# Several small moves around the attention pieces of a fused sliding-window attention and ELU feed-forward kernel

## The chip, the cores and the metric

One core of a Trainium2 chip runs the whole program. The metric is the device time of one execution in microseconds (us). PE is the matmul engine, DVE the vector engine, ACT the scalar engine, POOL the GpSimd engine and SP the engine that issues the DMAs. [...]

## The reference

```python
# attention: q, k, v are [8 batches, 8 heads, 576, 64]
scores = (q @ k.T) / sqrt(64)
mask   = (0 <= rel < 32)                                # heads 0 to 3
       | (0 <= rel < 128 and rel % 4 == 0)              # heads 4 to 7
attn   = softmax(where(mask, scores, -1e9)) @ v
x      = attn as [4608, 512]                            # 8 batches x 576 rows, 8 heads x 64
# feed-forward
h = x @ w_in                                            # [512, 2048]
g = where(h > 0, h, exp(min(h, 0)) - 1)                 # ELU
out = g @ w_out                                         # [2048, 512]
```

The inputs are float32. The feed-forward products split each operand in a rounded part and a rest (names `xh`, `xl`, `gh`, `gl`, `wh`, `wl`) and add three matmuls.

## The kernel before

**Chunks.** The 4608 rows of x are nine chunks of 512 (`c` = 0 to 8). Chunks 0 to 2 go through sixteen blocks of 128 hidden columns (`f`); I write (c, f) for a place there. Chunks 3 to 8 (`CS` = 3) do the first product by a scheme with seven products for eight: four groups `g` of seven steps `s`, numbered `step = 7 * g + s`.

**A block of chunk 1 or 2.** PE does the first product of block f into a PSUM bank `h0` (12 matmuls of 512 columns), then the second product of block f - 2 into the banks `o_ps` (12 matmuls). There is one `h0`: the next first product waits until ACT has copied `h0` away. The ELU of the block is ACT copy of `h`, ACT exp, ACT relu, DVE scalar_tensor_tensor (e), ACT cast to `gh`, DVE subtraction to `gl`. The last two, "the rest" of the ELU (lines 577 and 578), are asked for one block later (`before`, `steps`). `gl` is read by every third matmul of the second product two blocks on.

**Attention pieces.** Attention for later batches is cut into pieces of two head pairs. A scores piece (`scores_piece`) is 72 small matmuls, which appear as 144 in the trace, into the banks `a_ps0`, `a_ps1` and `h1`. After a third of them ACT reads one column of `h1` into `nothing` (line 481): the second head's scores into that bank wait for this read. Then DVE adds masks, takes the maximum, subtracts; ACT takes exp; DVE sums, scales, and makes six transposes into `pt` for each head pair. An outputs piece (`outputs_piece`) multiplies `pt` with v, one head pair after the other, and ACT copies the outputs to `x32`. In chunks 1 and 2 the pieces stand after the blocks in `WHEN` (scores, outputs, scores, outputs); after block (2, 14) stands one scores piece for chunk 3's group; in chunks 3 to 8 the pieces stand at the steps in `PIECES`.

**What sets the order.** A scheduler orders the instructions of each engine when the program is built, from the order of the code and its own estimate of time; `tc.issue_after` adds an edge. What goes through `vec`, `act` or `inorder` keeps its order in the code: all matmuls, and DVE and ACT from block (2, 14) on. For batches up to `CS` the softmax goes through plain `nc.vector` and `nc.scalar`, and the scheduler places it; for later ones its steps are spread by hand (`work`, `SPARE`). `split_late` (lines 180 and 182) casts and subtracts weights once a block in chunk 1, `combine` (lines 230 to 237) prepares weights for chunk 3 at the places in `COMBINE`. `fifo` and `pop(n)` hold and issue the second products from chunk 3 on; `FIRST_POPS` and `POPS` say how many at a step.

**Shared small buffers.** Four buffers `e` of 128x512 serve the ELU, the output rows (`store`, line 600), and the casts of `combine`; a buffer is free again when its last reader, or the DMA that stores it, is done. `gl` has two buffers, `gh` three.

Of the kernel before, what the change touches and what calls it, by code (L numbers as in the profile page):

```python
# [18 lines left out]
B, H, S, D = 8, 8, 576, 64  # L19
# [5 lines left out]
G = 32  # L25
QB = 3 * G
NU = S // QB
NPAIR = H // 2
NA = 3
GU = QB // G  # L30
# [16 lines left out]
STORED = "A11 A12 S2 S4 S3 S1 A22".split()  # L47
MOVING = "B11 T2 T3 B21 T1 T4 B22".split()
POPS = (3, 4, 0, 4, 0, 5, 0)
FIRST_POPS = (2, 2, 1, 2, 1, 1, 2)  # L50
TODO = [t.split() for t in ("u1 exp0< relu0< rest1< w0", "u2 elu0< cast0< w1", "u3 rest0< w2", "C11 w3", "C22 w4", "C21 exp1 relu1 w5 push1", "elu1 C12 cast1 w6 push0")]
SPARE = ((0.9, 0.3, 1.0, 0.9, 1.2, 2.2, 0.3), (0.9, 0.9, 0.0, 1.6, 2.2, 1.0, 0.3), (0.9, 0.9, 2.2, 1.2, 2.0, 2.4, 0.3), (0.6, 0.6, 0.0, 0.3, 0.6, 1.2, 0.3))
OPERANDS = [t.split() for t in ("", "cast:B11 make:T1", "rest:B11", "make:T2 cast:T2", "rest:T2", "make:T3", "cast:T3 rest:T3",
                                "cast:B21 rest:B21", "make:T4 cast:T1", "rest:T1 cast:T4", "rest:T4 cast:B22", "rest:B22", "", "")]
WHEN = {1: (0, 6, 7, 13), 2: (1, 6, 7, 12)}
EARLY = 0.0
LAST = 14
OPER = 12
PLAIN = ("a5", "a-1'")
COMBINE = {(1, 11): 0, (1, 13): 1, (1, 15): 2, (2, 1): 3, (2, 4): 4, (2, 6): 5, (2, 9): 6, (2, 11): 7}  # L60
PIECES = {9: ("S", 2, 1), 14: ("O", 0, 1), 21: ("O", 2, 1), 23: ("S", 0, 2)}

TINY = float(np.array([0x38000000], np.uint32).view(np.float32)[0])
# [3 lines left out]
def body(ctx: ExitStack, tc: tile.TileContext, q, k, v, masks, w_in, w_out, out):  # L67
# [311 lines left out]
    def exponentials(b, hp, places, sm=None):  # L379

        if sm is None:
            sm = ap.tile([QB, 2 * NU, 2 * G], F32, name="sm", bufs=1)
            last = masks_added(hp, places, sm)
            if b == 1:
                masked.append(last.ins)
        nmx = ap.tile([QB, 2 * NU], F32, name="nmx", bufs=4)
        sums = ap.tile([QB, 2 * NU], F32, name="sums", bufs=4)
        nc.vector.tensor_reduce(out=nmx, in_=sm, op=ALU.max, axis=mybir.AxisListType.X)
        if b == 1:

            maxima.append(nc.vector.tensor_scalar(out=nmx, in0=nmx, scalar1=-0.125, scalar2=None, op0=ALU.mult).ins)
            for u in range(NU):
                exponential(u, sm, nmx, sums)
        else:
            nc.vector.tensor_tensor(out=sm, in0=sm, in1=nmx.unsqueeze(2).broadcast_to([QB, 2 * NU, 2 * G]), op=ALU.subtract)
            nc.scalar.activation(out=sm, in_=sm, func=AF.Exp, scale=0.125)
            nc.vector.tensor_reduce(out=sums, in_=sm, op=ALU.add, axis=mybir.AxisListType.X)
        return b, hp, sm, nmx, sums

    def probabilities(b, hp, sm, nmx, sums):  # L400

        if b == 1:

            for u in range(NU, 2 * NU):
                exponential(u, sm, nmx, sums)
        normalise(nc.vector, sm, sums, lambda ins: ins)
        tr = transposed()
        for c in range(GU):
            for r in range(2):
                ks, cs, rs = slice((c + r) * G, (c + r + 1) * G), slice(c * G, (c + 1) * G), slice(r * G, (r + 1) * G)  # L410
                last_transpose[b] = nc.vector.transpose(out=tr[ks, :, cs], in_=sm[cs, :, rs]).ins
        return b, hp, tr

    def three():

        return banks() + [ps_h.tile([P, TC], F32, name="h1")]
# [49 lines left out]
    def scores_piece(b, hps):  # L466

        s = three()

        def place(j, h, n0, n1):  # L470

            bank, o = (s[h], n0 + j * NU) if j == 0 or n0 < 2 else (s[2], n0 - 2 + h * 4)
            return bank[:, o * 2 * G:(o + n1 - n0) * 2 * G]

        qk = [qk_of.pop(b * NPAIR + hp) for hp in hps]

        one, other = [(0, n) for n in range(NU)], [(1, n) for n in range(NU)]
        for i, (first_head, second_head) in enumerate(zip(other[2:] + other[:2] + one, other[:2] + one + other[2:])):
            if i == 4:

                nc.scalar.copy(out=nothing, in_=place(1, 0, NU - 1, NU)[:QB, 2 * G - 1:])
            for c in range(GU):
                for h, (j, n) in enumerate((first_head, second_head)):
                    score(place(j, h, n, n + 1), *qk[j], h, n, c)
        groups = [[[(n0, n1, place(j, h, n0, n1)) for n0, n1 in (((0, NU),), ((2, NU), (0, 2)))[j]] for h in range(2)] for j in range(2)]
        if b <= CS:
            made = [probabilities(*exponentials(b, hp, groups[j])) for j, hp in enumerate(hps)]
        else:
            made = later_probabilities(b, hps, groups)
        for hp in hps:  # L490
            load_qk(b * NPAIR + hp + 2)
        return made
# [205 lines left out]
    def pop(n):  # L698
        for _ in range(min(n, len(fifo))):
            second_product(*fifo.pop(0))  # L700
# [30 lines left out]
    def combined_chunk(c):  # L731

        x_ps = y_ps = None
        halves = lambda x: x.rearrange("p (i t) -> p i t", i=2)
        for g in range(NG):
            base = (c - CS) * NG * 7 + g * 7
            for s in range(7):
                step = 7 * g + s
                what, hp, ahead = PIECES.get(step, ("", 0, B))
                if what and c + ahead < B:  # L740
                    if what == "S":
                        if hp:
                            work(100.0)
                        made[hp] = scores_piece(c + ahead, (hp, hp + 1))
                    else:
                        if hp:
                            work(100.0)
                        outputs_piece(made.pop(hp))
                        if hp == 0:
                            side.extend(held)  # L750
                            held.clear()
                load_combined(base + s + RING)
                if s == 0:
                    x_ps = ps_h.tile([P, TC], F32, name="h0")
                    live["before"], live["now"] = live.get("now"), (c, g, [sets.pop(0), sets.pop(0)])
                    sets.extend(live["now"][2])
                if (c, g, s) == (CS, 1, 0):
                    moving["temporary"] = late
                if s == 3:
                    y_ps = ps_h.tile([P, TC], F32, name="h1")  # L760
                product(base + s, x_ps if ORDER[s] in ("A11", "S2", "S3", "A22") else y_ps, s in (0, 3, 4))
                for what in TODO[s]:
                    if what in ("u1", "u2", "u3"):
                        live[what] = fp.tile([P, TC], F32, name="e")
                        act.copy(out=live[what], in_=x_ps)
                    elif what == "C21":
                        act.copy(out=rows[1][:, :, :HT], in_=halves(x_ps))
                    elif what[0] == "C":
                        to, u = {"C11": (rows[0][:, :, :HT], "u1"), "C22": (rows[1][:, :, HT:], "u3"), "C12": (rows[0][:, :, HT:], "u2")}[what]
                        vec.tensor_tensor(out=to, in0=halves(y_ps), in1=halves(live.pop(u)), op=ALU.add)  # L770
                    elif what[0] == "w":
                        work(SPARE[g][s])
                    elif what[0] == "p":
                        push(int(what[4:]))
                    else:
                        activation(what)
                if g == NG - 1 and c + 1 < NCH:
                    for what in OPERANDS[s]:
                        moving_operand(c + 1, what, vec, act)
                if g == 0:  # L780
                    for what in OPERANDS[7 + s]:
                        moving_operand(c, what, vec, act)
                pop((FIRST_POPS if (c, g) == (CS, 0) else POPS)[s])

    def second_attention():

# [80 lines left out]
    for c in range(CS):  # L867
# [14 lines left out]
        for f in range(NF):  # L882
# [20 lines left out]
            if c == 0 and f >= NF - 2:  # L903
                ends.append(elu_steps(gemm1(c, f)))
                if f == NF - 2:
                    next(ends[0])
                    first_late = split_steps(0, 0, 2, [slots(*a) for a in LATE[0]], vec, act)
                else:
                    for _ in first_late:
                        pass  # L910
                    next(ends[0])
            else:
                steps = elu(gemm1(c, f), c, f, before, *strict)
                g = next(steps)
                if c == 0 or c == CS - 1 and f >= NF - 3:
                    if g[1] is not None:
                        next(steps)
                    steps = None
                before = steps
                pend.append((c, f, g))  # L920
            if c == 1:
                keep_plain(f)
            if (c, f) == (0, 0):
# [103 lines left out]
```

## Time and profile before

| what | value |
|---|---|
| median of 3 runs | 884.86 us (884.64 to 887.34) |
| the profiled execution's own time | 884.33 us |
| its span, first to last instruction | 882.5 us |
| mean granted PE clock | 0.994 |
| busy in the span: PE, DVE, ACT | 863.4, 609.1, 455.7 us |

PE is busy in nearly all of the span, but its matmuls are pipelined and their ends are modelled, so the times to look at are those between the starts of matmuls, and the few places where PE stands. A row of the timeline gives start, duration, engine, line, operation, names (out<-in), sizes, and in brackets the idle time ahead of it with what ended it.

### The profile page before, as it was taken

To read this page: it belongs to the slowest core of one execution; us is meant where nothing else is said; L and a number is where in the kernel's file an instruction comes from. 1 tells how busy PE (TensorE), PEld (TensorE's weight loads), DVE (VectorE), ACT (ScalarE), POOL (GpSimd) and SP (SyncE) were. 2 spreads that over 40 slices of the span, in tenths; PEclk is the share of its full clock that TensorE was granted. 3 is DMA by queue.
4 is the path that set the end of the run, shared out by engine and by line. 5 is a ranking of instruction groups with operands and counts; after the bars stand their busy time and mean duration, and the time that the engine had idled before them with its cause. 6 is when DMAs were issued, how large, how long until landed. Compare 5 with 4: busy or idle time off the path is not lost. (4 is left out here: it accounts for less than half of the span.)

```text
span 882.5 us, 17850 instructions
## 1 busy us (share of the span) xinstructions
PE 863.4 (98%) x7424; PEld 725.6 (82%) x7424; DVE 609.1 (69%) x921; ACT 455.7 (52%) x783; POOL 6.0 (1%) x12
## 2 busy tenths in 40 slices
PE   6999999999999999999999999999999999999998
PEld 5545678878878888898989998889898989998996
DVE  6999998867588968966867597748775533453332
ACT  3666667645655565434554455446454453454334
POOL 2000000000000000000000000000000000000000
PEclk7999999999999999999999999999999999999999
DMA  9996335123454657757575657656665565557541
GB/s 342 387 356 245 123 121 187 48 92 120 155 199 156 198 165 226 227 187 236 176 258 188 225 178 248 219 182 223 196 199 167 167 215 176 183 175 224 175 144 48
DMA packets 66961, 170.68 MB, mean 193 GB/s; under 512 B 6752, under 2 KB 21440, under 8 KB 66880
## 3 DMA queue, kind: packets, MB, share of 16 engines
q1 hardware_dynamic: 66880, 169.54, 58.9%
q8 instruction: 59, 0.97, 0.4%
q14 instruction: 22, 0.18, 0.1%
HBM read 141.20 MB, written 28.31 MB: 192 GB/s over the span
## 5 line engine op out<-in xcount | busy, mean ns | idle before, releaser
L104 PE MATMUL h<-xh,r 128*128 128x256 f32 (+1 forms) x984 | 223.2, 308 | 2.1 <-PE h L104 1.0
L104 PEld LDWEIGHTS h<-xh,r 128*128 128x128 f32 x984 | 165.1, 191 | 13.9 <-PE h L104 1.2
L104 PE MATMUL h<-xl,r 128*128 128x256 f32 (+1 forms) x492 | 142.7, 307 | 0.6 <-DVE xl L424 0.6
L104 PE MATMUL o_ps<-a,r 128*128 128x512 f32 x480 | 117.0, 391 | 0.0
L424 DVE SCALAR_TENSOR_TENSOR a-1_3249<-a-1_3249,a 128x1024 f32<-128x1024 f32 x48 | 58.7, 1223 | 83.2 <-ACT a L424 83.1
L424 DVE TENSOR_TENSOR a-1_3249<-h,e 128x512 f32<-128x512 f32 x72 | 49.7, 690 | 82.5 <-PE h L104 81.1
L104 PEld LDWEIGHTS h<-xl,r 128*128 128x128 f32 x492 | 93.8, 191 | 9.0 <-issue 2.1
L104 PEld LDWEIGHTS o_ps<-a,r 128*128 128x128 f32 x480 | 87.6, 188 | 16.5
L104 PE MATMUL o_ps<-a,gh 128*128 128x512 f32 x248 | 89.4, 463 | 0.0
L424 ACT COPY e<-h 128x512 f32<-128x512 f32 x72 | 42.2, 586 | 80.8 <-PE h L104 65.7
L104 PE MATMUL h<-a,r 128*128 128x256 f32 x576 | 77.5, 284 | 0.0
L104 PEld LDWEIGHTS h<-a,r 128*128 128x128 f32 x576 | 74.0, 191 | 3.0
L424 ACT COPY a-1_3249<-h 128x512 f32<-128x512 f32 x24 | 14.1, 587 | 109.6 <-PE h L104 109.6
L104 PEld LDWEIGHTS o_ps<-a,gh 128*128 128x128 f32 x248 | 46.3, 188 | 24.2 <-issue 17.2
L424 ACT ACTIVATE a<-a 128x1024 f32<-128x1024 f32 (+1 forms) x56 | 57.0, 1030 | 1.3
L104 PE MATMUL o_ps<-r,r 128*128 128x512 f32 x212 | 56.8, 391 | 0.0
L104 PE MATMUL o_ps<-a,a 128*128 128x512 f32 x216 | 54.6, 391 | 0.0
L424 ACT ACTIVATE a<-a-1_3249 128x1024 f32<-128x1024 f32 x48 | 51.0, 1063 | 1.3 <-DVE a-1_3249 L424 0.5
L104 PEld LDWEIGHTS o_ps<-a,a 128*128 128x128 f32 x216 | 39.4, 188 | 7.4
L424 ACT CAST r<-a-1_3249 128x1024 fp32r<-128x1024 f32 x32 | 33.6, 1050 | 22.2 <-DVE a-1_3249 L424 22.1
L104 PEld LDWEIGHTS o_ps<-r,r 128*128 128x128 f32 x212 | 38.7, 188 | 7.3
L424 DVE TENSOR_TENSOR r<-a-1_3249,r 128x1024 fp32r<-128x1024 f32 x32 | 39.0, 1218 | 6.7 <-ACT r L424 6.2
(179 smaller groups left out, 1431.6 us busy)
## 6 DMA issues: line engine op xcount, KB each, us to landing
r<-combined SPq DMA_DIRECT2D x168, 512.0 KB, 4.1
vt<-v SPq DMA_DIRECT2D x30, 384.0 KB, 4.2
kt<-k SPq DMA_DIRECT2D x30, 304.0 KB, 4.9
out<-e SPq DMA_DIRECT2D x35, 256.0 KB, 3.1
qt<-q SPq DMA_DIRECT2D x30, 288.0 KB, 4.0
r<-w_in SPq DMA_DIRECT2D x16, 512.0 KB, 7.6
r<-w_out SPq DMA_DIRECT2D x16, 512.0 KB, 8.0
combined<-a SPq DMA_DIRECT2D x20, 256.0 KB, 2.9
```

What stands on the lines that cost most here:

```text
L104: return inorder(nc.tensor.matmul(*args, **kw))
L424: return lambda *args, **kw: inorder(getattr(self.eng, name)(*args, **kw))
```

## The change

Five edits, all of order and place; the arithmetic is the same.

1. `WHEN[2]` (1, 6, 7, 12) becomes (2, 6, 7, 12): the first scores piece of chunk 2 stands one block later. In chunk 3 the piece at step 9 moves to step 10, ahead of the product that writes `h1`, with two pops behind it, and the pops of chunk 3's second group change from (3, 4, 0, 4, 0, 5, 0) to (3, 4, 3, 3, 0, 1, 0).
2. For batches up to `CS` a generator `softmax` writes the six transposes as three and three, spread over the blocks behind the piece.
3. At the blocks in `WHEN` the ELU's rest is asked for at once, ahead of the piece, not one block later.
4. In chunk 3, group 0, step 4, the subtraction `rest:B22` (it makes `xl3`) is asked for ahead of that step's other work.
5. The read of `nothing` between the heads goes to DVE, in order, for batches over `CS`: at (2, 14) and in chunks 3 to 6.

```diff
-FIRST_POPS = (2, 2, 1, 2, 1, 1, 2)
+FIRST_POPS = (2, 2, 1, 2, 1, 1, 2), (3, 4, 3, 3, 0, 1, 0)
-WHEN = {1: (0, 6, 7, 13), 2: (1, 6, 7, 12)}
+WHEN = {1: (0, 6, 7, 13), 2: (2, 6, 7, 12)}
+FIRST_PIECES = {10: ("S", 2, 1), 14: ("O", 0, 1), 21: ("O", 2, 1), 23: ("S", 0, 2)}
 PIECES = {9: ("S", 2, 1), 14: ("O", 0, 1), 21: ("O", 2, 1), 23: ("S", 0, 2)}
+    def softmax(b, hp, places, tr):
+        _, _, sm, _, sums = exponentials(b, hp, places)
+        normalise(nc.vector, sm, sums, lambda ins: ins)
+        yield
+        for c in range(GU):
+            for r in range(2):
...
+                last_transpose[b] = nc.vector.transpose(out=tr[ks, :, cs], in_=sm[cs, :, rs]).ins
+                if (c, r) == (1, 0):
+                    yield
+        yield
...
-                nc.scalar.copy(out=nothing, in_=place(1, 0, NU - 1, NU)[:QB, 2 * G - 1:])
+                (vec.tensor_copy if b > CS else nc.scalar.copy)(out=nothing, in_=place(1, 0, NU - 1, NU)[:QB, 2 * G - 1:])
...
-            made = [probabilities(*exponentials(b, hp, groups[j])) for j, hp in enumerate(hps)]
+            trs = [transposed() for _ in hps]
+            made = [(b, hp, tr) for hp, tr in zip(hps, trs)]
+            one, other = [softmax(b, hp, groups[j], trs[j]) for j, hp in enumerate(hps)]
+            next(one)
+            spread.extend(((one,), (one, other), (other,), (other,)))
...
+                        if c == CS and hp:
+                            pop(2)
...
+                if (c, g, s) == (CS, 0, 4):
+                    moving_operand(c, *OPERANDS[7 + s], vec, act)
...
-                pop((FIRST_POPS if (c, g) == (CS, 0) else POPS)[s])
+                pop((FIRST_POPS[g] if c == CS and g < 2 else POPS)[s])
...
+                if steps is not None and f in when:
+                    next(steps)
+                    steps = None
...
+            for steps in spread.pop(0) if spread else ():
+                next(steps)
```

What the built programs then issue, at three places. The numbers of buffers differ between the two programs, and lines behind the edits have moved by up to twenty.

**DVE after block (1, 0).** `e_1373` is that block's ELU and `gl_1380` its rest, `sm_14..` is the first head pair's softmax, `a7` and `a6` are weight rests of `split_late`. Before:

```order
L573 SCALAR_TENSOR_TENSOR e_1373<-h_1374,e_1373 128x512
L375 TENSOR_TENSOR sm_1471<-a_ps1_1396,masks_sb_76 96x384
L375 TENSOR_TENSOR sm_1471<-a_ps0_1395,masks_sb_76 96x384
L388 TENSOR_REDUCE nmx_1474<-sm_1471 96x12
L395 TENSOR_TENSOR sm_1471<-sm_1471,nmx_1474 96x768
```

Now:

```order
L593 SCALAR_TENSOR_TENSOR e_1373<-h_1374,e_1373 128x512
L598 TENSOR_TENSOR gl_1380<-e_1373,gh_1379 128x512
L376 TENSOR_TENSOR sm_1473<-a_ps1_1398,masks_sb_76 96x384
L183 TENSOR_TENSOR a7_1493<-a1_521,a7_1493 128x1024
L183 TENSOR_TENSOR a6_1546<-a1_521,a6_1546 128x1024
L376 TENSOR_TENSOR sm_1473<-a_ps0_1397,masks_sb_76 96x384
L389 TENSOR_REDUCE nmx_1476<-sm_1473 96x12
L396 TENSOR_TENSOR sm_1473<-sm_1473,nmx_1476 96x768
```

The ELU's rest and two weight rests now stand ahead of the second mask and the subtraction; on ACT the exp of `sm` still stands ahead of the copy of the next block's `h0`.

**ACT around the moved scores piece of chunk 2.** `h_2489` is block (2, 2), `e_2488` and `gh_2496` its ELU, `e_2457` the last of four output rows that are copied and stored here, `e_2465` and `e_2470` casts of `combine`. Before, behind block (2, 1):

```order
L572 ACTIVATE e_2426<-e_2426 128x512
L600 COPY e_2451<-o_ps_1605 128x512
L481 COPY nothing_78<-h1_2477 96x1
L600 COPY e_2457<-o_ps_1609 128x512
L236 CAST e_2465<-a5_2125 128x512
```

Now, behind block (2, 2):

```order
L620 COPY e_2457<-o_ps_1603 128x512
L237 CAST e_2465<-a5_2125 128x512
L578 COPY h_2489<-h0_2475 128x512
L597 CAST gh_2434<-e_2426 128x512
L237 CAST e_2470<-a5_2125 128x512
L583 ACTIVATE e_2488<-h_2489 128x512
L592 ACTIVATE e_2488<-e_2488 128x512
L597 CAST gh_2496<-e_2488 128x512
L497 COPY nothing_78<-h1_2518 96x1
L397 ACTIVATE sm_2592<-sm_2592 96x768
```

The read moved from behind block (2, 1)'s relu to behind block (2, 2)'s cast to `gh`. `e_2488` takes the buffer of `e_2457`.

**DVE at the scores piece after (2, 14).** `e_3315` is the block's ELU, the second row its rest. Before:

```order
L424 SCALAR_TENSOR_TENSOR e_3315<-h_3316,e_3315 128x512
L424 TENSOR_TENSOR r3_1227<-e_3315,gh_3321 128x512
L424 TENSOR_TENSOR a5_2125<-h1_3326,masks_sb_76 96x256 x2
L424 TENSOR_TENSOR a5_2125<-a_ps0_3324,masks_sb_76 96x128
L424 TENSOR_TENSOR a5_2125<-a_ps1_3325,masks_sb_76 96x128
```

Now:

```order
L440 SCALAR_TENSOR_TENSOR e_3315<-h_3316,e_3315 128x512
L440 TENSOR_TENSOR r3_1227<-e_3315,gh_3321 128x512
L440 COPY nothing_78<-h1_3326 96x1
L440 TENSOR_TENSOR a5_2125<-h1_3326,masks_sb_76 96x256 x2
L440 TENSOR_TENSOR a5_2125<-a_ps0_3324,masks_sb_76 96x128
```

The read, which stood on ACT between the block's exp and its relu, stands on DVE behind the block's whole ELU.

More of the change, by code (lines that the diff above doesn't have):

```diff
@@ L412, in probabilities @@
         return b, hp, tr
+    spread = []
+    def softmax(b, hp, places, tr):
[4 more added lines that the diff above has]
+            for r in range(2):
+                ks, cs, rs = slice((c + r) * G, (c + r + 1) * G), slice(c * G, (c + 1) * G), slice(r * G, (r + 1) * G)
+                last_transpose[b] = nc.vector.transpose(out=tr[ks, :, cs], in_=sm[cs, :, rs]).ins
+                if (c, r) == (1, 0):
+                    yield
+        yield
     def three():
@@ L738, in combined_chunk @@
                 step = 7 * g + s
-                what, hp, ahead = PIECES.get(step, ("", 0, B))
+                what, hp, ahead = (FIRST_PIECES if c == CS else PIECES).get(step, ("", 0, B))
                 if what and c + ahead < B:
@@ L779, in combined_chunk @@
                         moving_operand(c + 1, what, vec, act)
-                if g == 0:
+                if g == 0 and (c, s) != (CS, 4):
                     for what in OPERANDS[7 + s]:
                         moving_operand(c, what, vec, act)
-                pop((FIRST_POPS if (c, g) == (CS, 0) else POPS)[s])
+                pop((FIRST_POPS[g] if c == CS and g < 2 else POPS)[s])
     def second_attention():
```

## The prediction, made before the changed kernel was run

> **What bounds the kernel now.** I read the page first: busy time per engine and the DMA issues.
>
> ```profile
> PE 863.4 (98%) x7424; PEld 725.6 (82%) x7424; DVE 609.1 (69%) x921; ACT 455.7 (52%) x783; POOL 6.0 (1%) x12
> ...
> out<-e SPq DMA_DIRECT2D x35, 256.0 KB, 3.1
> ```
>
> PE is the bound, and the change adds and removes no matmul. So only places where PE stands can pay, and every new wait of PE is lost in full. Then the waits of PE behind the first 100 us (engine and tile, who released it; total, times, longest):
>
> ```profile
> PE h L104 <- ACT nothing L481: 1.5, 3, 0.9
> PE o_ps L104 <- DVE gl L578: 1.3, 1, 1.3
> PE h L104 <- PE h L104: 1.0, 1, 1.0
> PE h L104 <- issue: 0.9, 1, 0.9
> PE h L104 <- DVE xl L424: 0.6, 1, 0.6
> ```
>
> Seven waits. The timeline of PE has the instructions that ended them:
>
> ```profile
> 195.47 0.50 PE L104 MATMUL o_ps<-a,gl 128*128 128x512 f32 x1 [1.29 <-DVE gl L578]
> ...
> 248.24 0.39 PE L104 MATMUL h<-xh,r 128*128 128x512 f32 x1 [0.95 <-issue]
> ...
> 323.35 0.24 PE L104 MATMUL h<-kt,qt 64*32 64x64 f32 x1 [0.23 <-ACT nothing L481]
> ...
> 343.99 0.39 PE L104 MATMUL h<-xl,r 128*128 128x256 f32 x1 [0.63 <-DVE xl L424]
> ...
> 358.86 0.36 PE L104 MATMUL h<-xh,r 128*128 128x256 f32 x1 [1.01 <-PE h L104]
> ...
> 450.39 0.24 PE L104 MATMUL h<-kt,qt 64*32 64x64 f32 x1 [0.92 <-ACT nothing L481]
> ...
> 635.82 0.24 PE L104 MATMUL h<-kt,qt 64*32 64x64 f32 x1 [0.40 <-ACT nothing L481]
> ```
>
> The brackets understate the loss. A matmul of 512 columns is drawn 0.39 long, but the next starts 0.23 later (below, 12 of them take 249.60 to 252.32, 2.72); the modelled end hides 0.16 of each wait, 0.2 for the small matmuls of scores. So the losses are 1.45, 1.11, 0.43, 0.79, 1.17, 1.12 and 0.60: 6.7 us in all, the most that this change can win. Now what it puts in their place, place by place.
>
> **The piece after (2, 14): +2.8.** The old order, with the durations of one ELU:
>
> ```profile
> 321.90 0.24 PE L104 MATMUL h<-kt,qt 64*32 64x64 f32 x1
> ...
> 322.00 0.59 ACT L424 COPY h<-h 128x512 f32<-128x512 f32 x1 [1.08 <-PE h L104]
> 322.62 0.63 ACT L424 ACTIVATE e<-h 128x512 f32<-128x512 f32 x1
> 323.16 0.14 ACT L481 COPY nothing<-h 96x1 f32<-96x1 f32 x1
> 323.28 0.63 ACT L424 ACTIVATE e<-e 128x512 f32<-128x512 f32 x1
> ...
> 323.94 0.69 DVE L424 SCALAR_TENSOR_TENSOR e<-h,e 128x512 f32<-128x512 f32 x1 [2.29 <-ACT e L424]
> ...
> 324.67 0.62 ACT L424 CAST gh<-e 128x512 fp32r<-128x512 f32 x1 [0.76 <-DVE e L424]
> ...
> 325.32 0.69 DVE L424 TENSOR_TENSOR r<-e,gh 128x512 fp32r<-128x512 f32 x1 [0.69 <-ACT gh L424]
> ```
>
> Scores start at 321.90 and PE restarts at 323.35 after losing 0.43, so the read is wanted 1.0 us after the scores start. Now the read stands on DVE behind the ELU's last subtraction, which ends at 326.01. It can end at about 326.15 (0.14, the price on ACT; DVE's isn't shown, and 0.1 either way changes little). PE restarts 2.8 later than before. ACT is relieved of 0.14 only, so the ELU isn't earlier. Queued behind the read on DVE are the masks, wanted by nobody on PE soon. This is the surest term; it would shrink only if DVE's order were another.
>
> **The piece after (1, 0): +1.5.**
>
> ```profile
> 138.10 1.05 ACT L180 CAST r<-a 128x1024 fp32r<-128x1024 f32 x1
> ...
> 139.99 0.58 ACT L558 COPY h<-h 128x512 f32<-128x512 f32 x1
> 140.32 1.22 DVE L182 TENSOR_TENSOR a<-a,a 128x1024 fp32r<-128x1024 f32 x1
> ...
> 142.53 1.01 DVE L375 TENSOR_TENSOR sm<-a_ps,masks_sb 96x384 f32<-96x384 f32 x2
> ...
> 145.55 0.85 ACT L396 ACTIVATE sm<-sm 96x768 f32<-96x768 f32 x1 [3.62 <-DVE sm L395]
> ...
> 148.22 0.39 PE L104 MATMUL h<-xh,r 128*128 128x512 f32 x1
> ```
>
> The second mask ends at 143.54, the exp of `sm` starts 2.01 later, and behind it ACT copies the next `h0`, which PE needs at 148.22. Now a cast of 1.05 goes behind the copy, so that starts at about 139.05; with the durations above the ELU is 141.7, `gh` 142.3, `gl` 143.0, first mask 143.5. Then stand two weight rests of 1.22, to 145.9, and the second mask, to 146.35. Exp at 148.35, its end 149.2, the copy's end 149.75: 1.5 after PE wants it. Lower end 0, if the weight rests come so that the mask isn't behind them; upper 2.4, both rests in full.
>
> **The piece after (1, 7): -0.8.** The 1.45 goes, since three transposes no longer stand ahead of `gl`. The read now follows the block's `gh`: I put 0.2 on it (one small read and a gap), and 0.5 on one `gl` (0.69) that the order still leaves behind three transposes; both between 0 and 0.7.
>
> **The moved piece, after (2, 2): +2.0.**
>
> ```profile
> 243.90 0.24 PE L104 MATMUL h<-kt,qt 64*32 64x64 f32 x1
> ...
> 246.14 0.59 ACT L600 COPY e<-o_ps 128x512 f32<-128x512 f32 x1 [1.20 <-DMA out<-e]
> ...
> 248.53 1.18 ACT L236 CAST e<-a 128x512 fp32r<-128x512 f32 x2 [1.80 <-DMA out<-e]
> ...
> 249.60 0.61 PE L104 MATMUL o_ps<-r,gh 128*128 128x512 f32 x2
> ...
> 252.32 0.39 PE L104 MATMUL h<-xh,a 128*128 128x512 f32 x1
> ```
>
> Two sets of 12 matmuls, 5.44, now stand ahead of the scores: they start at 249.35, and the read is wanted at 250.35. ACT waits for the stores of output rows until 248.53. From there the order says cast (0.6), copy of `h0` (0.59), `gh` (0.62), cast (0.6), exp, relu, the ELU on DVE, `gh`, read: with 0.63, 0.63, 0.69, 0.62, 0.14 and the gaps of the rows above, 253.5. PE would stand 3.1. In exchange the gap of 1.11 at 248.24 goes: nothing on another engine ended it, it stands six matmuls behind the 144 small ones of a piece, and that piece is no longer there. If it appeared behind the new place, the standing PE would cover it. Ends: -1.1 (read in time) and +3.1 (the gap stays as well).
>
> [...]
>
> **The outputs piece after (2, 6): +0.6.** The last six transposes of that softmax, the stretch of DVE from the first mask to their end, and the outputs:
>
> ```profile
> 245.40:273.34 27.94, 23.92 (x44) 1.00 0.43 148
> ...
> 269.86 3.48 DVE L411 STREAM_TRANSPOSE pt<-sm 32x384 f32<-32x384 f32 x6
> ...
> 274.52 1.87 PE L104 MATMUL a_ps<-pt,vt 128*64 128x96 f32 x40
> ```
>
> Transposes end at 273.34, 1.2 ahead of the outputs. The read moves from some 1 us behind 243.90 to 253.5 while the outputs move by 2.0: 6.6 less room. DVE idled 4.0 in this stretch (27.94 less 23.92). Missing: 6.6 - 1.2 - 4.0 = 1.4 for the first products, about 1 less for the second pair, which alone reads these transposes, and 0.5 more for the part of the idle that is waiting for the softmax's own exp: 0.9. A wait of 0.3 in the blocks between, caused by transposes ahead of a `gl`, goes. Ends 0 and 2.0.
>
> **The piece after (2, 7): +1.2.**
>
> ```profile
> 283.06 0.15 ACT L481 COPY nothing<-h 96x1 f32<-96x1 f32 x1 [1.05 <-PE h L104]
> ```
>
> ACT waited 1.05 for PE here and read at once. Now the read stands behind this block's ELU and `gh`: 0.69 + 0.62 and gaps, 1.4 later by the rows above, less a tenth or two of slack. Ends 0 and 2.
>
> **Chunk 3: -0.8.**
>
> ```profile
> 354.39 3.48 DVE L424 STREAM_TRANSPOSE pt<-a 32x384 f32<-32x384 f32 x6
> ...
> 360.00 1.21 DVE L424 TENSOR_TENSOR r<-a-1_3249,r 128x1024 fp32r<-128x1024 f32 x1
> ```
>
> `rest:B22` moved ahead removes the 0.79. At 358.86 the product that writes `h1` waited for masks behind six transposes; the piece moved ahead of it, and the pops, remove 1.17. But the read, now on DVE, stands behind the transposes (357.87) and a rest of 1.21: it ends near 359.3, and the scores, 24 matmuls of 256 columns later (2.7 by half of the 0.23 each), want it at 358.2. New wait 1.1. Ends -2.0 and +1.2.
>
> **Chunks 4 and 6: -1.7.** The 1.12 and 0.60 were reads on ACT behind its long weight casts. DVE was idle there:
>
> ```profile
> 451.22 0.75 DVE L424 TENSOR_TENSOR a<-h,masks_sb 96x256 f32<-96x256 f32 x2 [4.36 <-PE h L104]
> ```
>
> **At no cost.** The transposes written three and three, and the ELU's rest asked for earlier, are the same instructions; what they displace is in the places above, and elsewhere DVE and ACT, busy 69% and 52%, cover it. POOL's queue is unchanged. SP's queue keeps its number of issues; loads of q and k for the next piece wait for the scores that free their buffer, so they come with the moved piece some 8.5 us later (5.4 and the 3.1 of waiting), and two loads of v change places with writes of `combine`. The next scores piece reads q and k some 30 us on (283.06), the outputs piece reads v at 274.52, so with a landing near the 3.1 of the stores nothing shows. With that cover gone, one landing of about 3 us would.
>
> **Sum.** 2.8 + 1.5 - 0.8 + 2.0 + 0.6 + 1.2 - 0.8 - 1.7 = +4.8. The profiled execution took 884.33, 0.53 below the median 884.86 of the runs shown; so 889.13 against that execution, and 889.6 beside the median.
>
> **Rivals.** A, not slower: the stores of chunk 1's output rows land sooner, so that ACT isn't behind in chunk 2. It decides at the moved piece: the exp there must start by 247.3 for the read to be in time at 250.35. For it: the landing varies with the DMA traffic, and the store's median of 3.1 from issue is short. Against: both copies and casts of the rows above waited for stores. Price: the 3.1 goes, the outputs' 0.9 and the 1.2 at (2, 7) too: 4.8 - 5.2 = -0.4, 883.9 by the profile, 884.5 beside the median.
>
> B, faster: the new waits don't exist, because the scheduler's order differs on the chip from my placement and each read is met; then all seven losses go, -6.7: 877.6, or 878.2 beside the median. For it: all of them come from my adding of rows along the order, with gaps of under 0.1 between instructions, and most are no longer than the 1 to 2 us by which such a sum can be off. Against: the read behind (2, 14)'s ELU is fixed in order, and its term doesn't hang on any sum.
>
> C, slower still: the moved pieces bring an "issue" gap like that at 248.24 where PE doesn't stand anyway, behind chunk 3's moved piece and behind the one after (2, 14). For it: the gap follows the small matmuls of a piece, and the other engines were not late there. Against: only one of the pieces of before shows it. Price: 1.11 twice, 891.3, or 891.8 beside the median.
>
> **How the numbers follow.** 0.54 for the forecast, 0.20 for A, 0.15 for B, 0.11 for C. The likeliest case's own range is 886.5 to 891.5: the ends of its unsure terms seldom fall together. The range, 883.0 to 892.5, holds A, the forecast and C, and leaves out B and a tail. 0.3%, about what can be told from no change, is 2.65 us: faster 0.15 (B), same 0.20 (A), slower 0.65 (the forecast and C). The forecast is 889.6 us.
>
> **What would show it.** Right: PE's waits for DVE `nothing`, near 2.8 us at (2, 14) and near 1 in chunk 3, for ACT `nothing` some 3 after (2, 2) and 1 after (2, 7), for ACT's copy of `h` at (1, 1); none at chunks 4 and 6, and no "issue" after (2, 1). Wrong: PE going through (2, 14)'s scores without a stop, or ACT reaching the exp of (2, 2) before 248.

## The result: 0.9% slower, and more than forecast

| kernel | median | runs |
|---|---|---|
| before | 885.69 us | 884.64 to 887.34, six |
| changed | 893.63 us | 892.18 to 894.93, six |

The ratio is 1.0087, 95% interval 1.0073 to 1.0102. The profiled execution of the changed kernel took 892.39, with a span of 890.6 against 882.5. The forecast was 889.6, the range ended at 892.5: the direction was right, the size too small by 4.

The waits of PE behind the first 100 us, of the changed kernel (engine and tile, who released it; total, times, longest; line 104 of before is 105 here, 481 is 497):

```profile
PE h L105 <- DVE nothing L440: 3.8, 2, 3.0
PE h L105 <- ACT nothing L497: 3.4, 2, 2.8
PE h L105 <- ACT h L578: 1.6, 2, 1.5
PE h L105 <- DVE a-1_3251 L440: 1.4, 1, 1.4
PE o_ps L105 <- DVE gl L598: 0.7, 1, 0.7
PE h L105 <- issue: 0.2, 1, 0.2
```

The reads of one column, `nothing`, cost 7.2 instead of 1.5. The instructions that ended these waits, in the timeline of PE:

```profile
150.72 0.50 PE L105 MATMUL h<-xh,r 128*128 128x512 f32 x1 [1.49 <-ACT h L578]
...
203.02 0.50 PE L105 MATMUL o_ps<-a,gl 128*128 128x512 f32 x1 [0.75 <-DVE gl L598]
...
256.26 0.24 PE L105 MATMUL h<-kt,qt 64*32 64x64 f32 x1 [2.82 <-ACT nothing L497]
...
257.81 0.63 PE L105 MATMUL h<-xl,a 128*128 128x512 f32 x1
258.24 0.63 PE L105 MATMUL h<-xh,a 128*128 128x512 f32 x1
...
289.98 0.24 PE L105 MATMUL h<-kt,qt 64*32 64x64 f32 x1 [0.57 <-ACT nothing L497]
...
333.21 0.24 PE L105 MATMUL h<-kt,qt 64*32 64x64 f32 x1 [3.01 <-DVE nothing L440]
...
369.00 0.24 PE L105 MATMUL h<-kt,qt 64*32 64x64 f32 x1 [0.78 <-DVE nothing L440]
...
382.98 0.30 PE L105 MATMUL h<-pt,vt 128*64 128x96 f32 x2 [1.38 <-DVE a-1_3251 L440]
```

Two of these have a counterpart before: the wait for `gl`, 1.29 one block earlier, and the read after (2, 14), 0.23. The other five old waits are gone. The two matmuls at 257.81 and 258.24 start 0.43 apart, where such matmuls start 0.23 apart elsewhere.

The order of the matmuls is the same but for the moved pieces, so the two traces can be laid side by side: the start of the same matmul in both, and the difference as it grows.

| stretch | forecast | measured |
|---|---|---|
| start, to 100 us | 0 | +1.1 |
| piece after (1, 0) | +1.5 | +1.2 |
| piece after (1, 7) | -0.8 | +0.2 |
| moved piece after (2, 2), outputs after (2, 6) | +2.6 | +3.3 |
| piece after (2, 7) | +1.2 | +0.8 |
| to (2, 14) | 0 | +0.4 |
| piece after (2, 14) | +2.8 | +2.7 |
| chunk 3 | -0.8 | +0.9 |
| chunks 4 and 6 | -1.7 | -1.9 |
| the rest | 0 | -0.7 |
| sum | +4.8 | +8.1 |

(The measured column sums to 8.0 by its rounding; the last matmul is 8.16 later.) The start is not the change's. The first scores, with the same instructions ahead of them, wait for a load of k: before, changed, and the changed kernel in another run.

```profile
5.60 1.52 PE L104 MATMUL a<-kt,qt 64*32 64x64 f32 x72 [1.60 <-DMA kt<-k]
```

```profile
6.60 0.67 PE L105 MATMUL a<-kt,qt 64*32 64x64 f32 x24 [2.58 <-DMA kt<-k]
```

```profile
5.63 1.52 PE L105 MATMUL a<-kt,qt 64*32 64x64 f32 x72 [1.41 <-DMA kt<-k]
```

In the two profiles of the changed kernel the scores behind this load start at 6.60 and 5.63, 0.97 apart, so the 1.1 at the start is not the change's in this profile. But other small waits vary as well: after_again, without that delay, is still 7.9 behind the kernel before at its last matmul, as the medians are. The two profiles of the same program drift against each other by 0.2 to 0.5 at several places, so a term is read from one profile to some 0.5 us, no better.

### The profile page after: what moved, and what is told of

It reads as the page before. It is cut to its first block, busy times and chain, and to the rows that moved or that the text cites. A ratio compares the mean times of both kernels' runs of the same rounds, so it can differ in the third digit from the quotient of the medians.

```text
span 890.6 us, 17850 instructions
## 1 busy us (share of the span) xinstructions
PE 865.0 (97%) x7424; PEld 726.9 (82%) x7424; DVE 611.8 (69%) x929; ACT 455.4 (51%) x775; POOL 6.0 (1%) x12
## 4 chain that ended last, share of the span: by engine, by line
PE 80%; DVE 12%; ACT 4%; issue 2%; DMA 1%; POOL 0%; SPq 0%; DVEq 0%; ACTq 0%
PE o_ps L105 38%; PE h L105 37%; PE a_ps L105 3%; DVE pt L425 2%; DVE nmx L389 1%; DVE e L593 1%; DVE sm L376 1%; DVE sm L307 1%; DVE sm L396 1%; DVE gl L598 1%; DMA kt<-k 1%; DMA out<-e 1%; ACT pt L362 0%; ACT h L578 0%; DVE a L183 0%
```

## The experiments

Each kernel but after_again was timed in five rounds beside the kernel before, and the ratio is to that. The medians stand beside different runs of the kernel before (884.64 to 885.69 us), so differences to the changed kernel are taken from the ratios, 8.85 us for 0.01; one of under 2 us is within their intervals. Three questions: does each wait count by itself, or does time saved come back as the next wait; what is chunk 3's wait at its outputs; what are the slow matmuls.

**undo_read**: the read stays on ACT where it cost.

```diff
-(vec.tensor_copy if b > CS else nc.scalar.copy)(out=nothing, ...
+(vec.tensor_copy if b > CS + 1 else nc.scalar.copy)(out=nothing, ...
```

> The changed kernel, with the read of the column between the heads back on ACT at (2, 14) and at chunk 3's moved piece; it stays on DVE in chunks 4 to 6. Theory of single waits (each wait read in the trace counts by itself): the 3.22 at (2, 14) falls to the 0.43 of before, the 0.99 at chunk 3's moved scores goes, the 1.59 at chunk 3's outputs stays: -3.8, so about 889.9 beside 893.6 for the change. Rival, give-back (DVE is late in chunk 3 by itself, and PE only meets the lateness at the next place): the outputs' wait of chunk 3 grows by what is saved, to 3 or more, and the time falls by less than 2.

888.73 us, ratio 1.0044 (1.0027 to 1.0060): 3.8 below the changed kernel (1.0087 less 1.0044), as the first theory had it. PE restarts at (2, 14) after 0.43 and in chunk 3 at once, and the outputs' wait stays at 1.5 (start to start), so nothing was given back there. (In the profiled execution the stand at (2, 2), which this edit doesn't touch, was 3.5 and the slow matmuls behind it twice as many, so that profile alone shows 3.3.) In the changed kernel the timeline of DVE at (2, 14) shows the cause as forecast:

```profile
331.02 0.69 DVE L440 SCALAR_TENSOR_TENSOR e<-h,e 128x512 f32<-128x512 f32 x1 [2.33 <-ACT e L440]
332.39 0.69 DVE L440 TENSOR_TENSOR r<-e,gh 128x512 fp32r<-128x512 f32 x1 [0.68 <-ACT gh L440]
333.00 0.15 DVE L440 COPY nothing<-h 96x1 f32<-96x1 f32 x1
```

The read takes 0.15 on DVE as on ACT; it is its place behind the ELU that costs.

**undo_rest**: the ELU's rest one block later again.

```diff
-                if steps is not None and f in when:
-                    next(steps)
-                    steps = None
```

> The changed kernel, with the ELU's rest asked for one block later again at the pieces of chunks 1 and 2. The order then has the read between the heads behind relu, not behind the cast to gh, at (2, 2) and (2, 7), only one weight rest ahead of the first mask at (1, 0) and none between the two masks, and the rest of (1, 7) behind five transposes. Single waits: 1.65 at (1, 1) goes, (2, 2)'s 3.03 falls to about 1.6, (2, 7)'s 0.77 goes, the wait for gl after (1, 7) is about 1.2 instead of 0.9: -3.5 to -4, so about 889.8. Rival, give-back: the waits come back as waits for gl or for ACT's copy of h0 in the next blocks, and the time falls by less than 2.

889.67 us, ratio 1.0057 (1.0044 to 1.0070), 2.7 below, less than the 3.5 to 4 expected. The wait at (1, 1) went, that of (2, 7) too, (2, 2)'s fell to 2.0. Part came back, at the outputs after (2, 6), which now wait for the transposes, and at (2, 14), where the same stand was followed by slow matmuls (below):

```profile
252.12 0.24 PE L105 MATMUL h<-kt,qt 64*32 64x64 f32 x1 [1.78 <-ACT nothing L497]
...
277.88 0.30 PE L105 MATMUL a_ps<-pt,vt 128*64 128x96 f32 x2 [1.91 <-DVE pt L425]
```

**undo_when**: chunk 2's first piece back behind (2, 1).

```diff
-WHEN = {1: (0, 6, 7, 13), 2: (2, 6, 7, 12)}
+WHEN = {1: (0, 6, 7, 13), 2: (1, 6, 7, 12)}
```

> The changed kernel, with chunk 2's first scores piece back behind block (2, 1). Single waits: the 3.03 and 0.36 at (2, 2) go; the gap put down to issue, 1.11, comes back behind the piece at (2, 1) if it belongs to the place of the instructions, as in the kernel before: -2.3, about 891.3. Rival: the gap belonged to something else of the kernel before and stays away: -3.4, about 890.2. Give-back: less than 1 falls, since ACT, late with output rows and casts, holds the next blocks.

890.22 us, ratio 1.0062 (1.0049 to 1.0074), 2.2 below by the ratios and 3.4 by the medians, so the time doesn't tell the first theory's 2.3 from the rival's 3.4. The trace does: the gap put down to issue came back, six matmuls behind the piece as before:

```profile
249.81 0.39 PE L105 MATMUL h<-xh,r 128*128 128x512 f32 x1 [1.06 <-issue]
```

The expectation left out the slow matmuls, and two errors cancel there: those behind (2, 2) went, and as many came behind (2, 14), both about 1.5. It left out too that the wait at (2, 7), some 0.8, would go, as it did.

**late_reads**: two parts alone, on the kernel before.

```diff
-nc.scalar.copy(out=nothing, ...
+(vec.tensor_copy if b > CS + 1 else nc.scalar.copy)(out=nothing, ...
...
+                if (c, g, s) == (CS, 0, 4):
+                    moving_operand(c, *OPERANDS[7 + s], vec, act)
...
-                if g == 0:
+                if g == 0 and (c, s) != (CS, 4):
```

> The kernel before with two parts of the change alone: the read between the heads on DVE in chunks 4 to 6 only, and the subtraction that makes xl3 asked for early in chunk 3. Single waits: the 1.12 and 0.60 of chunks 4 and 6 and the 0.79 at xl3 go, nothing comes: -2.5, about 883.2 beside 885.7 for the kernel before. Rival, give-back: DVE is later in chunk 3 behind the early subtraction, the masks of the piece there come later by up to 1.2, and DVE reads come late in one of chunks 4 to 6: 885 to 886.

883.38 us, ratio 0.9982 (0.9973 to 0.9991). That is 1.6 below the kernel before, with an interval of 0.8 to 2.4, and not the 2.5 of the first theory: the median comes out near its 883.2 only because the kernel before ran at 885.2 beside it, not at 885.7. Part was given back, as the rival had it in kind. In the trace the 1.12 and 0.60 are gone; of the 0.79 that the early subtraction saves, 0.56 comes back, at the product that writes `h1`, which waits 1.73 instead of 1.17. Another 0.5 is an "issue" gap at 408.56 that the kernel before has at under 0.1.

**no_combine**: less work on ACT ahead of the read at (2, 2).

```diff
-COMBINE = {(1, 11): 0, (1, 13): 1, (1, 15): 2, (2, 1): 3, ...
+COMBINE = {(1, 11): 0, (1, 13): 1, (1, 15): 2, (2, 3): 3, ...
```

> The changed kernel, with the work of combine that stood behind block (2, 1) (two casts on ACT, six operations on DVE, its DMAs) moved behind block (2, 3). The order then has on ACT ahead of the read at (2, 2) one ELU and no cast of combine, and the ELU's buffer e is one whose store was issued two rows earlier. ACT's lateness: copy of h0 at about 246.7 on the clock of the kernel before, the read done near 250.4, just when it is wanted: the 3.03 falls under 0.5, and with the stand the slow matmuls behind it go (another 1.5): -4 to -4.5, about 889.3 beside 893.6. Rival 1, the stand goes but the slow clock has another cause (the DMA traffic beside it): -2.8, about 890.8. Rival 2, the stores of output rows alone hold ACT: 2 or more of the 3.03 stays, 892 or more.

892.89 us, ratio 1.0094 (1.0078 to 1.0109), not below the changed kernel: my expectation failed. The stand at (2, 2) halved, to 1.6, and no slow matmuls follow it. But ACT was held by the stores themselves, as the second rival had it in part. The last output row's copy needs a buffer `e` whose store has not landed, in the changed kernel (first fence) and without the casts (second):

```profile
250.68 0.58 ACT L620 COPY e<-o_ps 128x512 f32<-128x512 f32 x1 [3.23 <-DMA out<-e]
...
253.49 0.63 ACT L583 ACTIVATE e<-h 128x512 f32<-128x512 f32 x1
...
256.06 0.15 ACT L497 COPY nothing<-h 96x1 f32<-96x1 f32 x1
```

```profile
249.26 0.59 ACT L620 COPY e<-o_ps 128x512 f32<-128x512 f32 x1 [2.77 <-DMA out<-e]
...
250.74 0.64 ACT L583 ACTIVATE e<-h 128x512 f32<-128x512 f32 x1
...
253.33 0.15 ACT L497 COPY nothing<-h 96x1 f32<-96x1 f32 x1
```

What was won went to two new waits, since the moved work now stands on DVE between the softmax's masks: 1.65 for `gl` at 270.44 and 1.23 for the transposes at 280.62 (start to start). Slow matmuls behind (2, 14), which the changed kernel doesn't have there, took another 1.3 (below).

```profile
270.44 0.50 PE L105 MATMUL o_ps<-a,gl 128*128 128x512 f32 x1 [1.49 <-DVE gl L598]
...
280.62 0.39 PE L105 MATMUL a_ps<-pt,vt 128*64 128x96 f32 x4 [1.03 <-DVE pt L425]
```

**undo_chunk3**: chunk 3's pieces and pops as before, reads on DVE.

```diff
-what, hp, ahead = (FIRST_PIECES if c == CS else PIECES).get(step, ...
+what, hp, ahead = PIECES.get(step, ...
...
-                        if c == CS and hp:
-                            pop(2)
...
-FIRST_POPS = ..., (3, 4, 3, 3, 0, 1, 0)
+FIRST_POPS = ..., (3, 4, 0, 4, 0, 5, 0)
```

> The changed kernel, with chunk 3's scores piece back at step 9 and the pops of its second group as before; the reads stay on DVE. Moved piece as the cause of the outputs' wait: the 1.59 goes; the read stands on DVE behind six transposes and PE stands about 2.5 in the scores instead of 0.99, and nothing at the product that writes h1: -0.1 to -0.5, about 893.3. Rival, the reads on DVE as the cause (all of DVE is later): the 1.59 stays, +1.2 to +1.5, about 895.

897.75 us, ratio 1.0142 (1.0120 to 1.0163), 4.9 above the changed kernel, which neither theory gave. The outputs' wait is gone, as the first said: it comes from the moved piece. But the read behind six transposes cost 3.34 start to start, not 2.5, since DVE came to the transposes later against the scores than before:

```profile
366.37 3.48 DVE L440 STREAM_TRANSPOSE pt<-a 32x384 f32<-32x384 f32 x6
369.88 0.15 DVE L440 COPY nothing<-h 96x1 f32<-96x1 f32 x1
```

Of the rest, about 1.6 are slow matmuls behind this stand, 1.3 those behind the stand at (2, 14), and another 1.5 a longer stand and more slow matmuls at (2, 2) (differences of the starts of the same matmuls). The read on DVE is thus worse without the moved piece, 3.34 instead of 0.99. The moved piece doesn't need the read on DVE: with the read on ACT (undo_read) PE doesn't stand in chunk 3's scores at all.

**chunk3_later**: the kernel before with both parts of late_reads, the moved piece and pops of chunk 3, and the outputs one step later.

```diff
-FIRST_PIECES = {10: ("S", 2, 1), 14: ("O", 0, 1), ...
+FIRST_PIECES = {10: ("S", 2, 1), 15: ("O", 0, 1), ...
```

> The kernel before with: reads on DVE in chunks 4 to 6, the early subtraction for xl3, and chunk 3's moved scores piece and pops, read on ACT; and its first outputs piece at step 15, not 14 (that is in neither kernel). The wait of chunk 3's outputs is for one addition on DVE that frees h1 and stands behind the softmax of the moved piece; one step of about 2.7 us later it should be done. Moved piece: 0.79, 1.17, 0.99 and 1.59 all stay away in chunk 3, and the 1.12 and 0.60 later: 885.3 less 3.7, about 881.6, and 1.7 less than the 883.4 of the kernel with the first two parts alone. Rival, give-back: DVE is late by itself in chunk 3, and PE waits 1 to 2 at the next product that needs h1 or at the second outputs piece: 883 to 884.

880.88 us, ratio 0.9956 (0.9943 to 0.9970), 3.9 below the kernel before where 3.7 was expected, and the fastest kernel of the study. With the piece moved, the 0.56 that late_reads gave back stays away too. The waits of PE that are left in it, of over 0.2:

```profile
PE o_ps L105 <- DVE gl L594: 1.3, 1, 1.3
PE h L105 <- issue: 1.1, 1, 1.1
```

**chunk3_alone** is the same with the outputs at step 14.

```diff
-FIRST_PIECES = {10: ("S", 2, 1), 15: ("O", 0, 1), ...
+FIRST_PIECES = {10: ("S", 2, 1), 14: ("O", 0, 1), ...
```

> The best kernel so far with chunk 3's first outputs piece back at step 14. The outputs' wait for the addition on DVE belongs to the two pieces standing four steps apart, not five: 1.5 to 1.6 comes back, 882.4 beside 880.9. Rival, it came from other delays of the changed kernel: within 0.5 of 880.9.

882.51 us, ratio 0.9980 (0.9971 to 0.9989). 2.1 above chunk3_later, and in the trace the one wait of 1.52 that the other lacks in chunk 3 is back:

```profile
372.64 0.39 PE L105 MATMUL h<-pt,vt 128*64 128x96 f32 x4 [1.31 <-DVE a-1_3249 L440]
```

What is waited for stands, in the changed kernel, behind the moved piece's softmax on DVE, which works there without a pause (DVE, the last three operations and the addition that frees `h1`):

```profile
379.97 0.23 DVE L440 RECIPROCAL sums<-sums 96x12 f32<-96x12 f32 x1
380.23 0.95 DVE L440 TENSOR_TENSOR sm<-sm,sums 96x768 f32<-96x768 f32 x1
381.11 1.22 DVE L440 SCALAR_TENSOR_TENSOR a-1_3251<-a-1_3251,a 128x1024 f32<-128x1024 f32 x1
382.24 0.68 DVE L440 TENSOR_TENSOR a-1_3251<-h,e 128x512 f32<-128x512 f32 x1
```

**undo_softmax**: the transposes six together again.

```diff
-            trs = [transposed() for _ in hps]
-            made = [(b, hp, tr) for hp, tr in zip(hps, trs)]
-            one, other = [softmax(b, hp, groups[j], trs[j]) for j, hp in enumerate(hps)]
-            next(one)
-            spread.extend(((one,), (one, other), (other,), (other,)))
+            made = [probabilities(*exponentials(b, hp, groups[j])) for j, hp in enumerate(hps)]
```

> The changed kernel, with the softmax of the pieces for batches up to 3 written in one as before, six transposes together, on DVE wherever the scheduler puts them. Single waits: the order has block (1, 8)'s gl behind six transposes and the second pair's masks, maximum and subtraction: its wait grows from 0.91 by about 1.7 (three transposes) to 2.6, the rest stays: +1.7, about 895.3. Rival, the transposes' place matters little because the rest asked for early decides: within 0.7 of 893.6.

894.28 us, ratio 1.0113 (1.0093 to 1.0133), 2.3 above the changed kernel where 1.7 was expected; the intervals overlap, so the time alone doesn't tell the two theories apart. The trace does on the mechanism: `gl` of (1, 8) waits 0.91 as before, and the six transposes of the second pair cost a second wait for a `gl`, 2.05 start to start, one block later than I had put it:

```profile
210.39 0.50 PE L105 MATMUL o_ps<-a,gl 128*128 128x512 f32 x1 [1.89 <-DVE gl L594]
```

**rests_early**: on chunk3_later, three rests asked for at once.

```diff
+                if steps is not None and c == 1 and f in (7, 8, 9):
+                    next(steps)
+                    steps = None
```

> The best kernel so far (reads on DVE in chunks 4 to 6, early subtraction for xl3, chunk 3's moved scores and pops with the read on ACT, outputs at step 15), and the rest of the ELU asked for at once in blocks (1, 7), (1, 8) and (1, 9) alone, with the transposes six together as before. The order has each gl ahead of the transposes. The 1.45 goes and the read at (1, 7) is 0.3 late: -1.1, about 879.8 beside 880.9. Rival, as in the changed kernel: gl of (1, 8) is late behind masks by about 0.9 and ACT's copy of h0 by 0.3, nothing is won: 880.9.

881.76 us, ratio 0.9967 (0.9956 to 0.9978): nothing won against 0.9956. The wait for `gl` is gone, and the read and ACT's copy of `h0`, behind the cast to `gh` that now stands ahead of them, wait instead:

```profile
185.48 0.24 PE L105 MATMUL h<-kt,qt 64*32 64x64 f32 x1 [0.47 <-ACT nothing L497]
...
198.34 0.50 PE L105 MATMUL h<-xh,r 128*128 128x512 f32 x1 [1.05 <-ACT h L574]
```

This is the rival's case, by the copy rather than by `gl`.

**after_again**: the changed kernel once more, unchanged, one run.

> The changed kernel once more, unchanged. If the slow matmuls depend on when a stand falls against a window that runs freely, this run shows them at another choice of the two stands of 3 us, at (2, 2) and (2, 14), and the time moves by 1 to 2 with it; if they belong to the place (the DMA traffic at (2, 2)), they stand behind (2, 2) alone again, with some 1.5 us lost.

892.10 us. The slow matmuls stand behind (2, 2) again and not behind (2, 14). By this run alone they would belong to the place; the other kernels say no. The granted clock in stretches of PE (stretch, length, PE busy and its count of matmuls, clock, DMA share, GB/s): the changed kernel at (2, 2) and at (2, 14), then at (2, 14) no_combine and undo_rest, then undo_softmax at (2, 2).

```profile
252.97:256.38 3.41, 0.59 (x57) 1.00 0.93 305
256.38:259.80 3.42, 3.42 (x52) 0.50 0.62 207
...
328.06:331.48 3.42, 2.14 (x103) 1.00 0.02 5
331.48:334.89 3.41, 1.68 (x51) 1.00 0.01 1
334.89:338.30 3.41, 3.41 (x18) 1.00 0.93 301
```

```profile
329.06:332.47 3.41, 0.40 (x38) 1.00 0.02 5
332.47:335.88 3.41, 3.41 (x52) 0.50 0.44 143
```

```profile
326.51:329.93 3.42, 1.44 (x49) 1.00 0.00 0
329.93:333.34 3.41, 3.41 (x10) 0.50 0.87 276
```

```profile
253.51:256.93 3.42, 1.26 (x109) 1.00 0.93 307
256.93:260.34 3.41, 3.41 (x52) 0.50 0.61 205
```

The stand at (2, 14) is 3.22 start to start in seven profiles. In three (the changed kernel twice, undo_softmax) the clock stayed, in four (undo_rest, undo_when, no_combine, undo_chunk3) it fell to 0.5. So neither the place nor the DMA traffic decides: half clock followed windows with a DMA share of 0.93 and of 0.00. In each of the thirteen profiles all changes of the granted clock lie whole multiples of 3.413 us apart; the stretches of this length I call windows, and the rows above are cut along them. A window ahead of half clock needn't be idle throughout: undo_rest's above has 1.44 of busy PE in 3.41.

In these profiles, where the windows fall against a stand tells the two outcomes apart. In the changed kernel the stand at (2, 14), 329.98 to 333.21, is cut by the boundary at 331.48, PE is busy for 2.14 and 1.68 in the two windows, and the clock stays. In no_combine the same stand fills one window, and the next runs at half clock. Over the seven profiles, the four with a window in which PE is busy for 1.44 or less are followed by half clock, the three with 1.68 or more in each window are not. At (2, 2) it is the same, with 1.26 or less in the five profiles with half clock and 2.04 or more in the two others that have the stand there. So the length of a stand alone doesn't tell: undo_softmax's of 2.37 lies in one window, and half clock follows. The limit isn't sharp by these busy times: one window with 1.62 (undo_chunk3, 368.30 to 371.71) was followed by half clock, one with 1.51 (undo_rest, 275.31 to 278.73) was not. No run moved a stand against the windows on purpose, and after_again didn't by chance: its boundary falls 1.67 us into the stand at (2, 14), that of the first profile 1.50.

## Why the prediction was right and wrong

The direction was right. The size was 3 too small (+4.8 against +7.9 by the medians and +8.1 in the profile), mainly by three steps of the prediction. Chunk 3's outputs piece isn't in the sum at all, and PE waits 1.6 there. "Every new wait of PE is lost in full" holds no price for what follows a wait, and the half clock behind (2, 2) took about 1.5 more. At (1, 7) 0.7 of the gain of 1.45 was forecast to come back, and 1.5 did. In this profile the 1.1 at the start adds to it, and smaller differences of both signs.

- **The piece after (2, 14), +2.8: right**, to 0.1, by its mechanism. undo_read takes it away.
- **The piece after (1, 0), +1.5: right**; 1.65 for the copy, less 0.28 by the earlier read. In the trace DVE does two weight rests (2.35) between the two masks, as the order said.
- **Chunks 4 and 6, -1.7: right**; in late_reads' trace the 1.12 and 0.60 go as well.
- **The moved piece, +2.0: the wait right, its price wrong.** The stand measured 3.03, forecast 3.1, and the gap of 1.11 went. The step that failed here is the first one, "every new wait of PE is lost in full", as if a wait cost its own length and no more: behind this one matmuls ran at half the clock (0.50 from 256.38 to 259.80), which cost about 1.5 more (some seven starts 0.2 late, and 0.36 at the first). I read ACT as held until the first cast; it is the output row's copy that the store holds.
- **The outputs after (2, 6), +0.6: measured 0** in the changed kernel, most likely since the 3 us for which PE stood, and the slow matmuls behind it, gave DVE the time. undo_rest and no_combine, with a shorter stand, show the wait at 2.1 and 1.2: the mechanism is there. That its size hangs on the stand alone isn't shown, since both also move work on DVE.
- **The piece after (2, 7), +1.2: measured 0.8**, right in kind.
- **The piece after (1, 7), -0.8: wrong, +0.2.** The 1.45 went, but `gl` of the next block was 0.9 late where I put 0.5, the read 0.3, and ACT's copy of `h0` another 0.3 late at 216, which I had not seen.
- **Chunk 3, -0.8: wrong, +0.9.** The 0.79 and 1.17 went and the read cost 0.99 (1.1 forecast). The term left out is the outputs piece at step 14, +1.6: I moved the scores piece in the order, but not its softmax on DVE, ahead of the addition that frees `h1`. chunk3_later, with the outputs one step on, has no such wait, and chunk3_alone, without that step, has it again. Another 0.39 is an "issue" gap behind the later scores piece at step 23; after_again, the same program, doesn't have it, so it is not the change's.
- The start, +1.1, is a run's own, not the change's.

Rival B was the farthest off. Rival C's gaps don't show where it put them: none stands behind chunk 3's moved piece or behind the one after (2, 14). The gap of 1.11 was rightly taken to go with the piece: it stands at 0.56 to 1.46 in the six kernels that have the piece behind (2, 1), and not in the others; in undo_rest and no_combine, where no slow matmuls could cover it behind (2, 2), the starts there are 0.23 apart from the third on. What the gap is, no run here shows.

## What to carry to other kernels

A read that lets the second half of a burst start belongs where the bank's reader has nothing else to wait for; being on an engine with idle time doesn't help when that engine's queue has the whole ELU ahead of it (2.8 us lost here, with DVE idle for 2.33 and 0.68 ahead of the ELU's two operations, against 1.7 won where DVE's queue was empty). When a piece of work moves, follow all that it issues down each queue to the next place where PE needs that engine: the scores piece was moved by one step, and its softmax was met four steps later, at 1.6. And where the bound is PE, a stand can cost more than its length: behind these stands of 2.37 us and more, where PE was busy for 1.44 us or less of one 3.41 us window, half clock followed, and took about 1.5 us more (2.4 where it lasted two windows).

## What the runs showed of the hardware that I had not expected

Between the first 100 us and the last matmul, half clock came in whole windows: ten stretches in eight profiles, eight of 3.41 us and two of 6.83, all on one grid per profile (starts of 512-column matmuls 0.427 apart, not 0.227). The same instructions with the same stand of 3.22 us got it or not, as the grid cut the stand. The "issue" gap six matmuls behind a burst of 144 small ones always came at the same instruction, but its length varied between 0.56 and 1.46 in six profiles.
